# Holding two early loads back behind a VectorE count, in a kernel of attention and feed-forward on one core

## The chip, the cores and the metric

The kernel runs on 1 core of one Trainium2 chip. The metric is the device time of one execution in microseconds (us); medians of several executions are given.

## The reference, cut to what matters

```python
mod = (silu(c) @ w_mod).reshape(1, 6, 1, -1)      # sa, ca, ga, sb, cb, gb
h = layernorm(x) * (1 + ca) + sa                  # x: 2048 x 1024
x = x + ga * attention(h, k_cache, v_cache, wq, wo)   # 32 heads of 128, last 512 keys
h = layernorm(x) * (1 + cb) + sb
x = x + gb * ((silu(h @ w_gate) * (h @ w_up)) @ w_down)
```

## The kernel before

TensorE does nearly all of the work. The tokens are handled in chunks of 512. The first attention phase is a loop over steps `i`, one head of one chunk at a time: project a query head, score the previous head, apply the probabilities of the one before. In between, the other engines prepare what comes later:

- **Tile transposes.** The normalised rows of the second chunk go through four DMA transposes on SyncE's queue (steps 3 to 5). At steps 8 and 9 VectorE *modulates* the result (gain and shift). The projection at step 9 is the first to read it.
- **Units.** The output projection is done later with seven products instead of eight, which needs differences of blocks of `wo`. They are prepared in sixteen units: GpSimd loads 512 KB, VectorE makes four differences (the *sums*, two at a tick), GpSimd stores them to memory.
- **Gate columns.** The columns of `w_mod` for `ga`, two loads of 1 MB, on SyncE's queue; the products of steps 12 to 14 read them.

```python
def unit_load(end):
    ...
    T.op(Q_of[slot][0], lambda: g.dma_start(dst, src), writes=[w.b_raw, w.b_s3])   # g: GpSimd

def unit_chain(k0, k1):
    unit_load(k1)
    unit_load(k1)
    yield
    for k in range(k0, k1):
        ...            # two pairs of sums, then the store and the load of the next unit

def pre0(i):
    ...
    if i in (7, 8):
        load_wga(i - 7)                                 # gate columns
    ...
    if i in (8, 9):
        for dt in range(4 * (i - 8), 4 * (i - 8) + 4):
            modulate(hT[1], B_hT[1], dt, 0, 0, B_mode, x1_tiles)
    if i < NQ0 + 1:
        if i % 2 == 0:
            qproj(NQ0 - 1 + i // 2)                     # ends in a copy-out on VectorE
    ...
    for n, tt in enumerate(NORMS.get(i, ())):           # steps 3, 4, 5
        norm_turn(1, tt, x1_tiles, (i + n) % 2)         # normalise, then DMA transpose
    ...
    if i == 5:
        bgx.append(row_task(sc_row, B_scr, sc_bf[:, :], B_sc))

def tick0(i):
    ...
    if i == 8:
        chain[0] = unit_chain(0, HP)
    if 8 <= i < NI - 8:
        unit_tick(i)                                    # skips every fourth step, and 21 to 24
```

`T.op` puts a wait into the issuing engine's stream only where a buffer was touched before. Nothing had touched the places of the first two units, so GpSimd issues their loads as soon as it has done its own earlier work (at 43.79 us in the profile below), however late "step 8" stands in the program.

The softmax here doesn't subtract the row's maximum and nothing guards it: scores larger than these inputs give would overflow.

## Time and profile before

| | before |
|---|---|
| time, median of the 3 executions at hand | 1162.26 us (1161.74 to 1162.92) |
| span of the profiled execution | 1159.8 us |
| TensorE busy | 1143.1 us, 99% |
| VectorE busy | 817.5 us, 70% |
| GpSimd busy | 68.8 us, 6% |

First the page of the kernel before: busy time per engine, and the chain of work that ended last, as shares of the span by engine and by line. Some 16.7 us of the span are idle TensorE; one per cent of the chain is a DMA of `nsc`, the normalised rows.

```profile
PE 1143.1 (99%) x7019; PEld 588.2 (51%) x7105; DVE 817.5 (70%) x1638; ACT 532.5 (46%) x745; POOL 68.8 (6%) x137
...
PE 94%; DVE 2%; DMA 1%; ACT 1%; issue 1%; SPq 0%; POOL 0%; DVEq 0%; ACTq 0%
PE ps L272 94%; ACT arena L805 1%; DMA arena<-nsc 1%; DVE arena L835 1%; DMA arena<-in_w_mod_dram 0%; DVE arena L906 0%; PE ps L276 0%; DVE st L413 0%; SPq L310 0%; DVE arena L432 0%; SPq L341 0%; DVE arena L852 0%; ACT tmp L743 0%; DVE arena L1563 0%; ACT L1548 0%
```

The table by windows of the same profile (busy us of each engine, with the number of instructions; then granted clock, share of the DMA engines' time, GB/s). Between 40 and 60 us TensorE lacks 3.3 us, and the DMA engines are full (share 1.00).

```profile
core 0: us, PE busy (x) PEld busy (x) DVE busy (x) ACT busy (x) POOL busy (x), PEclk, DMA share, GB/s
40.00:60.00 20.00, 16.68 (x163) 10.29 (x164) 13.51 (x33) 14.52 (x23) 3.82 (x7) 1.00 1.00 221
```

The timeline of the same profile from 42 to 56 us (start, duration, engine, line, operation, count; in brackets the idle time just before and what ended it). GpSimd issues the two unit loads at 43.79 us. SyncE issues the last two tile transposes from 43.23 us, that is the very last near 44.6 us. VectorE's first modulate (L432) waits 2.10 us for a transpose to land, the copy-out of the projection (L656) stands behind it, and TensorE waits 1.97 us for that.

```profile
43.23 2.70 SPq L454 DMA_TRANSPOSE arena<-nsc  x2
...
43.79 1.69 POOL L945 DMA_DIRECT2D arena<-in_A_wo_dram  x2
...
49.73 1.00 SPq L580 DMA_DIRECT2D arena<-in_w_mod_dram  x1
...
53.60 1.38 DVE L432 TENSOR_SCALAR arena<-arena,gain,mod_bf 128x512 f16<-128x512 f16 x4 [2.10 <-DMA arena<-nsc]
...
54.90 0.69 DVE L656 CAST arena<-ps 128x512 bf16<-128x512 f32 x1
...
55.64 0.60 PE L272 MATMUL ps<-arena 128*128 128x512 f16 x2 [1.97 <-DVE arena L656]
```

The view of the transposing line in the first 60 us gives the time from issue to landing of the four tile transposes: one took 9.0 us where the median is 3.3.

```profile
DMA to landing us min/median/max: 3.1/3.3/9.0
```

The DMA view of 47 to 51 us tells who had the engines (packets, MB, share of 16 engines): q0 is GpSimd's queue with the unit loads, q1 is SyncE's with the transposes.

```profile
q0 software_dynamic: 266, 0.96, 70.1%
q1 hardware_dynamic: 787, 0.20, 35.8%
```

### The profile page before, as it was taken

To read this page: it belongs to the slowest core of one execution; us is meant where nothing else is said; L and a number is where in the kernel's file an instruction comes from. 1 tells how busy PE (TensorE), PEld (TensorE's weight loads), DVE (VectorE), ACT (ScalarE), POOL (GpSimd) and SP (SyncE) were. 2 spreads that over 40 slices of the span, in tenths; PEclk is the share of its full clock that TensorE was granted. 3 is DMA by queue.
4 is the path that set the end of the run, shared out by engine and by line. 5 is a ranking of instruction groups with operands and counts; after the bars stand their busy time and mean duration, and the time that the engine had idled before them with its cause. 6 is when DMAs were issued, how large, how long until landed. Compare 5 with 4: busy or idle time off the path is not lost.

```text
span 1159.8 us, 18164 instructions
## 1 busy us (share of the span) xinstructions
PE 1143.1 (99%) x7019; PEld 588.2 (51%) x7105; DVE 817.5 (70%) x1638; ACT 532.5 (46%) x745; POOL 68.8 (6%) x137
## 2 busy tenths in 40 slices
PE   8899999999999999999999999999999999999999
PEld 5565556654446666556444444444444444444444
DVE  4758997657576777776567898767558777776536
ACT  3866777730117777787110344454110444544110
POOL 1200221000000111111000010000000000000000
PEclk9999999999999999999999999999999999999999
DMA  9878899966906898844865232333764424234443
GB/s 326 178 188 202 217 214 219 204 169 188 261 10 170 190 205 195 212 94 108 202 192 172 78 104 73 102 81 100 209 197 143 123 74 109 73 93 131 131 162 110
DMA packets 289941, 179.98 MB, mean 155 GB/s; under 512 B 130496, under 2 KB 278080, under 8 KB 289856
## 3 DMA queue, kind: packets, MB, share of 16 engines
q1 hardware_dynamic: 226880, 92.31, 35.8%
q10 hardware_dynamic: 54336, 55.05, 14.9%
q0 software_dynamic: 8640, 31.46, 9.1%
q8 instruction: 56, 0.92, 0.3%
q14 instruction: 29, 0.24, 0.1%
HBM read 128.45 MB, written 19.92 MB: 128 GB/s over the span
## 4 chain that ended last, share of the span: by engine, by line
PE 94%; DVE 2%; DMA 1%; ACT 1%; issue 1%; SPq 0%; POOL 0%; DVEq 0%; ACTq 0%
PE ps L272 94%; ACT arena L805 1%; DMA arena<-nsc 1%; DVE arena L835 1%; DMA arena<-in_w_mod_dram 0%; DVE arena L906 0%; PE ps L276 0%; DVE st L413 0%; SPq L310 0%; DVE arena L432 0%; SPq L341 0%; DVE arena L852 0%; ACT tmp L743 0%; DVE arena L1563 0%; ACT L1548 0%
## 5 line engine op out<-in xcount | busy, mean ns | idle before, releaser
L272 PE MATMUL ps<-arena 128*128 128x512 f16 (+2 forms) x6714 | 1135.4, 329 | 13.8 <-POOL arena L406 2.2
L272 PEld LDWEIGHTS ps<-arena 128*128 128x128 bf16 (+1 forms) x6800 | 578.0, 98 | 564.8 <-DVE arena L835 6.3
L805 ACT ACTIVATE arena<-ps 128x1024 bf16<-128x1024 f32 x256 | 261.3, 1021 | 45.9 <-PE ps L272 33.9
L838 ACT ACTIVATE tmp<-ps 128x512 f32<-128x512 f32 x167 | 99.7, 597 | 297.8 <-PE ps L272 283.7
L906 DVE TENSOR_TENSOR arena<-arena 128x512 f16<-128x512 bf16 x328 | 133.5, 420 | 3.0
L835 DVE TENSOR_TENSOR arena<-ps,tmp 128x512 bf16<-128x512 f32 (+1 forms) x134 | 91.9, 686 | 49.3 <-PE ps L272 37.8
L838 ACT ACTIVATE nsc<-ps 128x512 f32<-128x512 f32 x84 | 50.1, 596 | 93.2 <-PE ps L272 90.9
L827 DVE TENSOR_TENSOR arena<-ps,rl 128x512 f16<-128x512 f32 x128 | 88.5, 691 | 4.9 <-DVE rl L824 0.5
L835 DVE TENSOR_TENSOR arena<-ps,nsc 128x512 f16<-128x512 f32 x84 | 57.4, 687 | 41.2 <-PE ps L272 29.9
L824 DVE RECIPROCAL rl<-ps 128x4 f32<-128x4 f32 x128 | 23.1, 180 | 88.0 <-PE ps L272 87.0
L1548 ACT ACTIVATE arena<-arena 128x512 f16<-128x512 f16 x84 | 49.9, 624 | 32.4 <-DVE arena L835 32.4
L1044 DVE TENSOR_TENSOR arena<-arena 128x2048 f16<-128x2048 f16 (+3 forms) x56 | 56.2, 1013 | 9.3 <-PE ps L272 8.8
L1120 DVE TENSOR_TENSOR tmp<-ps,tmp 128x512 f32<-128x512 f32 x32 | 22.1, 690 | 57.0 <-ACT tmp L838 47.3
L838 ACT ACTIVATE arena<-ps 128x512 f32<-128x512 f32 x16 | 9.6, 597 | 89.0 <-PE ps L272 89.0
L956 DVE TENSOR_TENSOR arena<-arena 128x512 f16<-128x512 bf16 x120 | 48.0, 421 | 1.9 <-DMA arena<-in_A_wo_dram 0.8
L413 DVE BATCH_NORM_STATS2 st<-x_res 128x6 f32<-128x512 bf16 x58 | 39.6, 683 | 3.9 <-DMA x_res<-in_A_x_dram 3.7
L1563 DVE TENSOR_TENSOR arena<-arena 128x512 f16<-128x512 f16 x84 | 35.1, 418 | 0.3
L1121 DVE TENSOR_TENSOR tmp<-tmp,rowb 128x512 f32<-128x512 f32 (+1 forms) x49 | 33.6, 686 | 1.7
L427 DVE TENSOR_SCALAR nsc<-x_res,mv,rstd 128x1024 f16<-128x1024 bf16 (+1 forms) x30 | 16.2, 541 | 24.1 <-DMA arena<-nsc 23.4
L603 DVE SCALAR_TENSOR_TENSOR arena<-arena 128x1024 bf16<-128x1024 bf16 x24 | 29.2, 1217 | 0.0
L1122 DVE TENSOR_TENSOR arena<-tmp,x_res 128x512 bf16<-128x512 f32 (+1 forms) x33 | 22.3, 675 | 1.1
L835 DVE TENSOR_TENSOR arena<-ps,rowb 128x512 f16<-128x512 f32 x28 | 19.3, 690 | 3.9 <-ACT rowb L838 3.4
(87 smaller groups left out, 333.9 us busy)
## 6 DMA issues: line engine op xcount, KB each, us to landing
arena<-in_A_wq_dram SPq DMA_DIRECT2D x28, 512.0 KB, 5.2
arena<-wo_sum ACTq DMA_DIRECT2D x7, 2048.0 KB, 8.7
arena<-in_B_w_gate_dram SPq DMA_DIRECT2D x28, 512.0 KB, 4.1
arena<-in_B_w_up_dram SPq DMA_DIRECT2D x28, 512.0 KB, 4.9
arena<-wd_sum ACTq DMA_DIRECT2D x8, 1792.0 KB, 7.8
arena<-in_B_w_down_dram ACTq DMA_DIRECT2D x6, 1792.0 KB, 7.2
arena<-in_A_wo_dram POOLq DMA_DIRECT2D x16, 512.0 KB, 4.9
wo_sum<-arena POOLq DMA_DIRECT2D x16, 512.0 KB, 4.7
```

The lines of the kernel that those rows point to most:

```text
L272: T.op(PE, lambda: TE.matmul(out_ap, lhsT, rhs, start=start, stop=stop, skip_group_check=skip), reads=reads, writes=[bank_buf])
L413: T.op(DVE, lambda: V.bn_stats(st_[sl][:, hf * 6:hf * 6 + 6], x_res[:, t, hf * 512:hf * 512 + 512]), reads=[B_x[t]], writes=[B_st[sl]])
L805: T.op(ACT, lambda: A.activation(ex_s[es][:, 2 * kp:2 * kp + 2, :], banks2(SCB + 2 * kp), AF.Exp, scale=att_scale), writes=[PB[SCB + 2 * k ...
L827: T.op(DVE, lambda: V.tensor_tensor(o_s[os_].rearrange("p (a b) d -> p a b d", a=2), psap(PVB * 512, [[512, 2], [130, 2], [1, P]]), rlb, A ...
L835: T.op(DVE, lambda: V.tensor_tensor(out, bank(ba), other, ADD), reads=[ob2], writes=[PB[ba], ob])
L838: T.op(ACT, lambda: A.activation(dst, bank(bk), AF.Copy), writes=[PB[bk], db])
L906: T.op(st, lambda: eng.tensor_tensor(o, a, b, op), reads=rd, writes=[wr])
L956: T.op(DVE, lambda: V.tensor_tensor(o, a, b, SUB), reads=rd, writes=[wr])
L1044: T.op(DVE, lambda: V.tensor_tensor(o, a, b, SUB), reads=rd, writes=[sb])
L1121: T.op(DVE, lambda: V.tensor_tensor(tm, tm, rw, MULT), reads=[B_row[row]], writes=[tb])
L1548: T.op(ACT, lambda: A.activation(o, s_, AF.Silu), reads=[sb], writes=[ob])
L1563: T.op(DVE, lambda: V.tensor_tensor(gu[blk][:, p, :], o, s_, MULT), reads=[sb, ob], writes=[B_gu[blk][p]])
```

## The change

The intent: keep the unit loads off the DMA engines until the tile transposes are through. They get a wait for all the work that VectorE has been given by step 8, that is, for VectorE's instruction counter to reach that point (*the count* below); it is made with a stand-in buffer that nothing else touches. The sums start at step 12 instead of 9, so that they don't wait for the later loads, and the gate columns move one step.

```diff
-            def unit_load(end):
+            def unit_load(end, ahead=()):
...
-                T.op(Q_of[slot][0], lambda: g.dma_start(dst, src), writes=[w.b_raw, w.b_s3])
+                T.op(Q_of[slot][0], lambda: g.dma_start(dst, src), reads=ahead, writes=[w.b_raw, w.b_s3])
...
             def unit_chain(k0, k1):
-                unit_load(k1)
-                unit_load(k1)
+                after = _Buf("after")
+                after.last_write = (DVE, DVE.count)
+                unit_load(k1, [after])
+                unit_load(k1, [after])
...
-                if i in (7, 8):
-                    load_wga(i - 7)
+                if i in (8, 9):
+                    load_wga(i - 8)
...
                 if i == 8:
                     chain[0] = unit_chain(0, HP)
-                if 8 <= i < NI - 8:
+                    next(chain[0])
+                if 11 < i < NI - 4:
                     unit_tick(i)
```

## The prediction

> **What bounds it now.** The page's totals: TensorE is busy 1143.1 of 1159.8 us, so all its idle time is 16.7 us; the chain that ended last is 94% TensorE matmuls. Both builds issue the same TensorE instructions in the same order, so only idle time, mostly in the first 60 us, can be won.
>
> **What goes wrong now.** The table by windows gives 3.3 us of TensorE idle between 40 and 60 us, with the DMA engines fully busy. In the timeline:
> - GpSimd issues the first two unit loads (512 KB each) at 43.79 us, waiting for nothing but its own last rstd.
> - SyncE issues the last of four transposes of a normalised tile at 44.59 us. It lands at 53.57 us: 9.0 us, against a median of 3.3 us for these four.
> - VectorE's first modulate waits 2.10 us for it and starts at 53.60 us. Behind it in VectorE's order is the copy-out of a projection (54.90 us). TensorE needs that bank and waits 1.97 us, until 55.64 us: its longest wait after the start.
>
> The DMA view of 47 to 51 us shows what was in the way: GpSimd's queue moved 0.96 MB for 70% of the 16 engines' time, the transposes' queue 0.20 MB. [...] The first gate-column load (1 MB, issued 49.73 us) comes behind in the same place.
>
> **What the change does.**
> - It removes nothing and adds one wait on GpSimd. The unit loads go from 43.8 to about 54.5 us.
> - Gate-column loads move one step, to about 52 and 56 us. They are first needed at about 66 and 70 us and take 8 us; 3 MB in flight at 230 to 390 GB/s are through by about 63 us.
> - Sums: steps 12 to 54 keep theirs; the pairs of steps 9 and 10 (0.75 to 0.87 us each on VectorE) reappear in steps 56 and 57, where VectorE idles 0.8 and 2.25 us. The last store goes from 214.9 to about 223 us; the next load into its place is at 240 us.
> - The second chain's loads (345.2 us) also wait for VectorE, but their sums start only at 353.8 us.
>
> **Size.** Without unit loads in the way the last transpose should land near 48 to 49 us. VectorE can modulate from 51.5 us, when its previous copy ends; four modulates end near 52.9, the copy-out near 53.6, just as TensorE ends its run (53.67 us). The 1.97 us go; VectorE's 2.10 us are the same delay, not added. The second four modulates still pace the next projection (waits of 0.23 to 0.59 us), so I count 1.8 to 1.9 us. After 60 us each step is TensorE-bound at 3.49 us, so nothing gives this back. I allow 0.3 us either way for transfers shifted later. All of it is on the critical path, but it is 0.16% of the time.
>
> **Predicted:** 1160.4 us, range 1159.2 to 1161.8; faster by over 2% 0.01, within 2% 0.98, slower by over 2% 0.01.
>
> **What would show it.** Right: no DMA wait before the first modulate, no TensorE wait near 2 us between 50 and 60 us, the four transposes landing in under 5 us each, unit loads issued near 54.5 us, each reciprocal after 60 us about 1.9 us earlier. Wrong: the modulate still waits for the transpose, or TensorE waits anew near 66 to 73 us for gate columns or near 215 to 245 us.
>
> **What would make it wrong.** The delay could come from the transposes' own queue; the moved transfers now overlap fully and could hold the outputs' transposes until their four-deep ring stalls VectorE; late stores could delay the output projection.

## The result, and the profile after

The changed kernel takes 1160.1 us, median of 6 (1159.86 to 1160.62); the kernel before 1162.59 us, median of 6 (1161.74 to 1164.76). The ratio is 0.9976, 95% interval 0.9963 to 0.9989. A ratio here is the mean time of one kernel's fast runs over that of the other's of the same rounds, so not quite the ratio of the medians quoted. By the 2% rule this is "same"; the interval leaves no doubt that it is faster.

The page after: the DMA of `nsc` is gone from the chain. (TensorE's busy time is not comparable between these two profiles: the one before has 86 matmul records fewer. So the 16.7 us of idle TensorE before are too many; from the 10.0 us of the profile after and the span that is 1.5 us shorter, some 11.5 us are an estimate.)

```profile
PE 1148.3 (99%) x7105; PEld 588.0 (51%) x7105; DVE 817.4 (71%) x1638; ACT 532.7 (46%) x745; POOL 68.4 (6%) x137
...
PE 96%; DVE 2%; ACT 1%; DMA 1%; issue 0%; SPq 0%; ACTq 0%; DVEq 0%
PE ps L272 96%; ACT arena L805 1%; DMA arena<-in_A_wq_dram 1%; DVE arena L835 1%; DVE arena L906 0%; DVE st L413 0%; SPq L341 0%; SPq L310 0%; PE ps L276 0%; ACT arena L618 0%; DVE arena L852 0%; ACT tmp L743 0%; DVE arena L1566 0%; ACT L1551 0%; DVE arena L827 0%
```

The timeline after, 42 to 57 us. The unit loads go out at 55.13 us, after 11.09 us of waiting for VectorE. The modulate starts at 51.62 us without a wait, right behind VectorE's previous copy, the copy-out 2 us earlier than before. TensorE's only wait left at this place is 0.46 us, for the second four modulates.

```profile
43.36 2.68 SPq L454 DMA_TRANSPOSE arena<-nsc  x2
...
51.62 1.37 DVE L432 TENSOR_SCALAR arena<-arena,gain,mod_bf 128x512 f16<-128x512 f16 x4
52.51 0.45 SPq L580 DMA_DIRECT2D arena<-in_w_mod_dram  x1
...
52.91 0.68 DVE L656 CAST arena<-ps 128x512 bf16<-128x512 f32 x1
...
55.13 1.69 POOL L945 DMA_DIRECT2D arena<-in_A_wo_dram  x2 [11.09 <-DVE arena L827]
...
55.20 3.01 PE L272 MATMUL ps<-arena 128*128 128x512 f16 x21 [0.46 <-DVE arena L432]
```

Landing of the four tile transposes, and the DMA view of 47 to 51 us, of the changed kernel. GpSimd's queue is not there; the transposes have the engines.

```profile
DMA to landing us min/median/max: 3.1/3.3/3.4
```

```profile
q1 hardware_dynamic: 1345, 0.32, 62.0%
```

The gain can be counted between two reciprocals on VectorE that end a step: from that of step 7 to that of step 9 it is 49.99 to 59.94 us before, 9.95 us, and 50.20 to 58.42 us after, 8.22 us. That is 1.73 us won. From 58.42 us on, every step is as long as before: the span is shorter by 1.5 us, as the reciprocal is earlier by 1.52 us (the profiled execution after had started 0.2 us slower).

### The profile page after: what moved, and what is told of

It is laid out like the page before. It is cut to its first block, busy times and chain, and to the rows that moved or that the text cites. A ratio compares the mean times of both kernels' runs of the same rounds, so it can differ in the third digit from the quotient of the medians.

```text
span 1158.3 us, 18250 instructions
## 1 busy us (share of the span) xinstructions
PE 1148.3 (99%) x7105; PEld 588.0 (51%) x7105; DVE 817.4 (71%) x1638; ACT 532.7 (46%) x745; POOL 68.4 (6%) x137
## 4 chain that ended last, share of the span: by engine, by line
PE 96%; DVE 2%; ACT 1%; DMA 1%; issue 0%; SPq 0%; ACTq 0%; DVEq 0%
PE ps L272 96%; ACT arena L805 1%; DMA arena<-in_A_wq_dram 1%; DVE arena L835 1%; DVE arena L906 0%; DVE st L413 0%; SPq L341 0%; SPq L310 0%; PE ps L276 0%; ACT arena L618 0%; DVE arena L852 0%; ACT tmp L743 0%; DVE arena L1566 0%; ACT L1551 0%; DVE arena L827 0%
```

## The experiments

Twelve runs were made, each but one (c3) timed beside the kernel before on the same chip; c3 repeats the kernel before, d1 the changed kernel. Chips and rounds differ, so the kernel before has several medians. The clock column counts executions whose mean granted clock was below 1.0.

| run | what differs | median us (range) | before, same rounds | ratio (95%) | clock below 1.0 |
|---|---|---|---|---|---|
| the change | | 1160.1 (1159.86-1160.62) | 1162.59 | 0.9976 (0.9963-0.9989) | 0 of 6 |
| b1_loads_sums | change without the gate move | 1161.44 (1160.51-1165.26) | 1164.02 | 0.9983 (0.9967-1.0) | 1 of 6 |
| b2_gate_only | before with the gate move | 1164.78 (1161.7-1165.25) | 1164.02 | 1.0 (0.9983-1.0017) | 3 of 6 |
| b3_no_wait | change without the count | 1164.63 (1160.45-1165.85) | 1164.02 | 1.0002 (0.9985-1.002) | 5 of 6 |
| b4_loads_only | before with the count | 1161.31 (1160.8-1165.08) | 1164.02 | 0.9988 (0.997-1.0005) | 2 of 6 |
| c1_one_early | one unit load early, one held | 1160.71 (1160.25-1161.43) | 1164.09 | 0.9975 (0.9946-1.0004) | 0 of 4 |
| c2_sp_behind | both early, SyncE's queue | 1160.67 (1159.98-1163.67) | 1164.09 | 0.9978 (0.995-1.0005) | 0 of 4 |
| c3_before_again | kernel before, one look | 1164.53 | | | 1 of 1 |
| d1_after_again | the change again | 1160.27 (1159.91-1161.95) | 1164.32 | 0.9964 (0.9938-0.9991) | 0 of 6 |
| d2_row_later | change, row task later | 1162.04 (1160.08-1166.87) | 1164.32 | 0.998 (0.995-1.0009) | 1 of 6 |
| d3_mod_earlier | change, modulates earlier | 1159.33 (1158.8-1161.21) | 1164.32 | 0.9958 (0.9932-0.9984) | 0 of 6 |
| d4_row_mod | both | 1158.9 (1158.67-1160.65) | 1164.32 | 0.9953 (0.9924-0.9981) | 0 of 6 |
| e1_stall | change with an added stall | 1167.03 (1166.32-1168.57) | 1164.51 | 1.0029 (1.0014-1.0045) | 6 of 6 |

The theory, A: the two unit loads on GpSimd's queue hold up the tile transposes. Rivals: B, the first gate-column load does it; C, it is VectorE, relieved of the sums of steps 9 and 10; D, any megabyte moving at that time would do it.

### Without the gate move: b1_loads_sums

```diff
 (the change, but)
-                if i in (8, 9):
-                    load_wga(i - 8)
+                if i in (7, 8):
+                    load_wga(i - 7)
```

> The unit loads wait and the sums move, the gate columns stay one step earlier as before. Theory A (the two unit loads on GpSimd's queue held up the tile transpose): the four tile transposes land in under 4 us each, the first modulate has no DMA wait and starts near 51.6 us, TensorE has no wait near 2 us between 50 and 60 us; time 1.5 to 2.5 us below the kernel before, as the whole change. Rival B (the first gate-column load, issued near 50 us on the transposes' own queue, held it up): last transpose still lands after 53 us, time within 0.6 us of the kernel before.

All four transposes landed in 3.1 to 3.3 us, the modulate started at 51.85 us without a DMA wait, and TensorE had no wait of over 0.7 us but the one at the start. The two reciprocals stand at 50.42 and 58.65 us: 8.23 us, as with the whole change. B falls. The time is 2.6 us below the kernel before, by medians. Its full-clock executions (1160.51 to 1162.01) are somewhat above those of the change measured elsewhere; nothing in this profile shows a cost of the early gate load, and whether the move is worth a few tenths stays open.

### The gate move alone, and the change without the count: b2_gate_only, b3_no_wait

```diff
 (b2: the kernel before, but)
-                if i in (7, 8):
-                    load_wga(i - 7)
+                if i in (8, 9):
+                    load_wga(i - 8)
 (b3: the change, but)
-                unit_load(k1, [after])
-                unit_load(k1, [after])
+                unit_load(k1)
+                unit_load(k1)
```

> Only the gate-column loads one step later; unit loads early and sums as before. Theory A: the last tile transpose still takes 7 us or more, the modulate still waits 1 to 2.5 us, time within 0.6 us of the kernel before. Rival B: transposes under 5 us, no wait, 1.5 to 2.5 us faster.

> The whole change without the count: sums from step 12 and gate columns one step later, unit loads issued near 44 us again. Theory A: stall of the modulate is back (7 us or more to landing, 1 to 2.5 us waited), time within 0.6 us of the kernel before. Rival C (taking the sums of steps 9 and 10 off VectorE made room): time like the whole change, 1.5 to 2.5 us faster.

Both are as slow as the kernel before (ratios 1.0 and 1.0002; the medians are 0.8 and 0.6 us higher, where within 0.6 us was expected). In both the last transpose is late again. The timelines show the modulate's wait, 1.83 us in b2, and in b3 only 0.42 us, below the 1 us that the expectation asked for:

```profile
55.58 1.38 DVE L432 TENSOR_SCALAR arena<-arena,gain,mod_bf 128x512 f16<-128x512 f16 x4 [1.83 <-DMA arena<-nsc]
```

```profile
52.41 1.38 DVE L432 TENSOR_SCALAR arena<-arena,gain,mod_bf 128x512 f16<-128x512 f16 x4 [0.42 <-DMA arena<-nsc]
```

Landing times of the tile transposes, b2 first, then b3:

```profile
DMA to landing us min/median/max: 3.1/3.3/8.8
```

```profile
DMA to landing us min/median/max: 3.1/4.1/7.2
```

So B and C fall as explanations of the gain: with early unit loads, neither the gate move nor the moved sums gains anything. But b3's profiled execution took 1160.45 us, as fast as the change, while its other five took 1163.83 to 1165.85 us at a clock of 0.997 to 0.999. In that profile the two reciprocals are 8.27 us apart, hardly more than with the change (8.22): with both loads early, nearly nothing was lost. The stall that I took for a fixed cost is not fixed.

### The count alone: b4_loads_only

```diff
 (the change with the gate loads at steps 7 and 8, and)
-                if 11 < i < NI - 4:
+                if 8 < i < NI - 8:
```

> The count alone: unit loads near 55 us, sums still from step 9, gate columns as before. Theory A: the transpose stall goes, but the first sum at step 9 on VectorE now waits for a load that lands near 60 us, 1 to 5 us; some of it reaches TensorE at the next copy-out, so the gain is between 0 and 1.5 us and a wait of VectorE's sums on the load shows. If moving the sums was needless: no such wait, 1.5 to 2.5 us faster.

The transposes landed in 3.3 us at most and the modulate didn't wait. But the first sum, now at 61.32 us, waited 2.33 us for a load that had gone out at 54.79 us, and TensorE paid for most of it at the next copy-out. VectorE's line first, then TensorE's:

```profile
61.32 0.89 DVE L956 TENSOR_TENSOR arena<-arena 128x512 f16<-128x512 bf16 x2 [2.33 <-DMA arena<-in_A_wo_dram]
62.12 0.68 DVE L656 CAST arena<-ps 128x512 bf16<-128x512 f32 x1
```

```profile
62.86 5.40 PE L272 MATMUL ps<-arena 128*128 128x512 f16 x35 [1.32 <-DVE arena L656]
```

So in the profile the later start of the sums saves 1.3 us at this place. The times don't show it: b4's median is 2.7 us below the kernel before, more than the 0 to 1.5 us expected (1.4 us by the ratio, whose interval includes no gain), and in the same rounds b1, with the sums moved, has 1161.44 against b4's 1161.31. That the two edits belong together is shown by the waits, not by the times.

### Half the dose: c1_one_early

```diff
 (the change, but)
-                unit_load(k1, [after])
+                unit_load(k1)
                 unit_load(k1, [after])
```

> The changed kernel, but the first of the two unit loads is issued near 44 us as before and only the second waits. Half the dose. In the changed kernel the last tile transpose lands near 48.2 us and VectorE asks for it at 51.6 us, 3.4 us of slack; the two loads together moved for 4.6 us. Theory A: one load delays the landing by about 2 to 3 us, to 50 to 51.5 us, within the slack, so no wait or under 0.5 us, TensorE loses under 0.4 us and executions at full clock take 1160 to 1160.8 us. Rival (any early unit load brings the stall): the modulate waits 1 us or more and the time is that of the kernel before.

```profile
DMA to landing us min/median/max: 3.1/3.2/6.2
```

The last transpose took 6.2 us instead of 3.3, so one load alone delays it by 2.9 us. It hurts nobody: the modulate starts at 51.69 us without a wait. The delay of 2.9 us stays within the slack of 3.4 us and is free; in the kernel before, 5.7 us of delay (9.0 less 3.3) became 2.10 us of wait, about what exceeds the slack. (Two of the four executions, 1161.11 and 1161.43 us, lie above the 1160.8 us expected.)

### The same bytes on SyncE's queue: c2_sp_behind

```diff
 (the change; the first two unit loads leave unit_chain(0, HP) and go, at step 5, to SyncE)
                     norm_turn(1, tt, x1_tiles, (i + n) % 2)
+                if i == 5:
+                    unit_load(HP, sp=True)      # T.op(Q_sp[slot], lambda: SP.dma_start(dst, src), ...)
+                    unit_load(HP, sp=True)
```

> The changed kernel, but both unit loads go out early, near 46 us, on SyncE's own queue right behind the last tile transpose instead of on GpSimd's queue. Same bytes, same time, another queue. Theory A (two queues share the engines, packets of 4096 bytes against packets of 256): behind the transposes in their own queue the loads cannot pass them, all four land in under 4.5 us, the first modulate has no wait, executions at full clock within 0.7 us of the changed kernel's 1160.1 us. Rival D (a megabyte moving at that time is enough, whatever the queue): last landing 7 us or more, the modulate waits 1 us or more.

The DMA view of 47 to 51 us and the landings of this run:

```profile
q1 hardware_dynamic: 800, 1.10, 98.9%
```

```profile
DMA to landing us min/median/max: 3.1/3.3/3.4
```

1.10 MB moved in those 4 us, about as much as in the kernel before, and the tile transposes landed in 3.4 us at most; the modulate started at 51.48 us without a wait. D falls as it was put: a megabyte on its way early is harmless when it stands behind the transposes in their queue. But it is harmless because it moves later: in the DMA records the first packet of these loads starts at 47.20 us, and the last packet of the transposes ahead of them at 47.32 us. In the kernel before the two took turns, almost packet for packet: from 47 to 49.5 us, 193 packets of 4096 bytes on GpSimd's queue and 178 of 256 bytes on SyncE's. Two more limits: the loads here were issued at 45.95 us, 2.2 us later than before, and of four executions at full clock two were over the 0.7 us allowed, 1161.17 and 1163.67 us, which this work doesn't explain.

### The kernel before, a second profile: c3_before_again

> The kernel before, unchanged, for a second profile. Theory A says the early loads always reach the transposes, so the last tile transpose takes 6 us or more again; how much of it becomes a wait may vary, between 0.3 and 2.5 us, with where the instruction fetches near 51 us fall. If it lands in under 5 us here, the first profile was a stray and theory A is in doubt.

The landing, the waits of VectorE and TensorE, and the windows:

```profile
DMA to landing us min/median/max: 3.1/3.3/10.4
```

```profile
55.03 1.38 DVE L432 TENSOR_SCALAR arena<-arena,gain,mod_bf 128x512 f16<-128x512 f16 x4 [3.48 <-DMA arena<-nsc]
...
57.07 3.24 PE L272 MATMUL ps<-arena 128*128 128x512 f16 x9 [3.34 <-DVE arena L656]
```

```profile
58.00:59.00 1.00, 0.90 (x4) 0.30 (x3) 1.00 (x4) 0.00 (x0) 0.00 (x0) 0.84 1.07 342
59.00:60.00 1.00, 1.00 (x4) 0.39 (x3) 0.19 (x2) 0.00 (x0) 0.00 (x0) 0.50 1.14 371
...
61.00:62.00 1.00, 1.00 (x8) 0.72 (x7) 0.00 (x0) 0.91 (x2) 0.00 (x0) 0.50 1.03 365
62.00:63.00 1.00, 1.00 (x15) 0.84 (x13) 0.16 (x1) 0.92 (x1) 0.00 (x0) 0.95 0.51 113
```

The transpose took 10.4 us, 7.1 more than the median of the four. Some 3.4 us of that are slack (in the changed kernel it lands near 48.2 us and is asked for at 51.6); VectorE waited 3.48 us, more than the 2.5 us expected at most, and TensorE stood for 3.34 us. Then comes something that the first profile didn't have: the clock column goes to 0.50 and stays there for 3.4 us (the trace's clock record says 3413 ns). The step in which it falls, from VectorE's reciprocal at 56.93 us to the next at 62.84 us, takes 5.91 us, in the first profile 4.45 us (55.49 to 59.94): 1.46 us more. By an estimate, half of the 3413 ns, the lower clock costs 1.7 us. Wait and clock together, 3.34 + 1.7 less the 0.46 us that the changed kernel also waits, make 4.6 us; this span is 1162.7 us against 1158.3, 4.4 us.

### A stall without any transfer: e1_stall

```diff
 (the change, and in pre0)
+                if i == 8:
+                    for _ in range(7):
+                        stats(0, 0, 0)          # a needless bn_stats; its result is not used
```

> The changed kernel with seven needless bn_stats (0.61 us apart, 4.3 us) on VectorE ahead of the first modulate; loads untouched, result unchanged. A measured stall without any transfer in the way. TensorE should wait near 4.0 us for the copy-out (4.3 less 0.3 us of slack). Theory E (a wait of over some 3 us costs more than itself, because TensorE's granted clock then halves for one window, as in the second profile of the kernel before: 0.50 for 3.4 us after a wait of 3.34 us): executions show a mean clock of 0.999 or 0.998 and take 1165 to 1166.5 us, 1.7 us more than the wait alone; the profile shows clock 0.50 for about 3.4 us after 58 us. Without that effect: clock 1.0 and 1163.6 to 1164.6 us.

The result is still correct, and the four transposes landed in 3.4 us at most. TensorE's line of the timeline, then the windows:

```profile
58.70 11.62 PE L272 MATMUL ps<-arena 128*128 128x512 f16 x65 [4.74 <-DVE arena L656]
```

```profile
56.00:57.00 1.00, 0.00 (x0) 0.00 (x0) 0.97 (x4) 0.00 (x0) 0.00 (x0) 1.00 1.01 393
57.00:58.00 1.00, 0.00 (x0) 0.00 (x0) 1.00 (x5) 0.00 (x0) 0.00 (x0) 0.50 0.08 29
...
62.00:63.00 1.00, 1.00 (x4) 0.36 (x3) 0.67 (x1) 0.00 (x0) 0.00 (x0) 0.50 0.74 209
63.00:64.00 1.00, 1.00 (x7) 0.45 (x6) 0.03 (x1) 0.81 (x1) 0.00 (x0) 0.59 0.96 336
```

The wait is 4.74 us (seven instructions were 5.0 us, not 4.3 as I had estimated), and the mean clock was below 1.0 in all six executions, for two windows of 3.413 us in the profiled one (6827 ns in the record). The profiled execution's span is 6.4 us over that of the change (1164.7 against 1158.3; by medians of different rounds, 6.9). The wait gives 4.74 less 0.46, and, by the same estimate, half of the 5.1 us at half clock in which TensorE had work 2.6 us: 6.9, so 0.5 us more than the spans show. Theory E holds in that the clock fell, at double the windows foreseen. Two long stalls of TensorE, made in different ways (3.34 us in c3, 4.74 us here), cost more than themselves: the spans are 4.4 and 6.4 us longer than the changed kernel's.

How long is long? The clock records answer more than I had asked. In every kept profile that has one, the clock changes only at whole multiples of 3.413 us from the record's start (3413, 6827 and 51200 ns are 1, 2 and 15 of them), so the span can be cut into its windows. TensorE's busy time in the emptiest ones, and the clock that followed:

| profile | window, us | TensorE busy | clock in the next window |
|---|---|---|---|
| e1 | 53.58 to 57.00 | 0.39 us, 11% | 0.50 |
| c3 | 55.27 to 58.69 | 1.52 us, 44% | 0.50 |
| b2 | 8.80 to 12.21 | 1.62 us, 47% | 0.50 |
| e1 | 57.00 to 60.41, at half clock | 1.71 us, 50% | 0.50 |
| c3 | 51.86 to 55.27 | 1.87 us, 55% | 1.00 |
| kernel before | 54.24 to 57.65 | 1.91 us, 56% | 1.00 |
| d2 | 103.79 to 107.20 | 2.14 us, 63% | 1.00 |

Apart from the start and the end of the program, no other window is under 60% busy. So here a window in which TensorE was busy for half the time or less was followed by half clock, and one with 55% or more was not. In these records the clock goes by how much idle time falls into one window, not by how long the wait is: the 3.34 us of c3 were split over two windows, 55% and 44% busy, and only the second was followed by half clock. An estimate from these numbers: where TensorE is otherwise busy, a stall of under 1.5 us (45% of 3.413) should be safe, one of over 3.4 us not (at least 1.7 us of it, half, fall into one window), and in between it depends on where the windows fall. This was read from the records afterwards; no run was made to test it.

### Does this explain the times of the kernel before?

The kernel before had 40 timed executions with recorded clocks in four sets of rounds. In 28 of them the mean clock was below 1.0 (median 1164.7 us, 1163.25 to 1170.66), in 12 it was 1.0 (median 1161.6 us, 1160.25 to 1162.08). With b2 and b3, kernels with both unit loads early on GpSimd's queue had the lower clock in 36 of 52 timed executions; the kernels without had it in 4 of 50, the deliberate stall left out. That the lower clock comes from this stall was seen in one profile (c3) and made on purpose in another (e1); for the other executions it is inferred from the counts. It is not the only cause: the profiled execution of b2 had its halved window at the start of the kernel, 12.2 to 15.6 us, after the window of 47% in the table, in which no single wait was over 0.91 us. By the table, in the full-clock executions of the kernel before the stall should have been short, or split between two windows; the times alone can't tell which. Either way, comparing full-clock executions alone would leave out the part of the gain that comes through the clock.

### Further versions: d1 to d4

The changed kernel still has waits of TensorE of 0.24 and 0.51 us (for the exponentials on ScalarE at steps 6 and 7) and 0.46 us (for the second modulates).

```diff
 (d3 and d4)
-                if i in (8, 9):
-                    for dt in range(4 * (i - 8), 4 * (i - 8) + 4):
+                if i in (7, 8):
+                    for dt in range(4 * (i - 7), 4 * (i - 7) + 4):
 (d2 and d4)
-                if i == 5:
+                if i == 9:
                     bgx.append(row_task(sc_row, B_scr, sc_bf[:, :], B_sc))
```

> The changed kernel again, to stand beside the next three on one chip. All theories: four tile transposes under 5 us each, no DMA wait before the modulate, TensorE's remaining waits between 40 and 60 us near 0.2, 0.5 and 0.5 us; executions at full clock 1159.8 to 1160.8 us.

> The changed kernel with the row broadcast of silu(c) begun at step 9 instead of 5: its eight small ScalarE scalings (0.33 us each) no longer stand before the exponentials of steps 6 and 7, for which TensorE waits 0.24 and 0.51 us. Expected 0.5 to 1.2 us below the changed kernel at full clock, and these two waits gone or under 0.2 us; if ScalarE is not what paces these steps, no gain.

> The changed kernel with the modulates at steps 7 and 8 instead of 8 and 9. Transposes land near 48.2 us, the first modulate would start near 49.0 us in VectorE's idle 1.2 us of step 7, the second four near 51.6 us, so the projection at step 9 finds all of its input: the wait of 0.46 us and the small ones behind it go. Expected 0.4 to 0.9 us below the changed kernel at full clock; no gain if the transposes land later than 49 us.

> Both of the last two. Expected sum: 0.9 to 2.0 us below the changed kernel at full clock, near 1158.7 us, the fastest of all.

d1 confirms the change in other rounds, with 4.1 us between the medians this time (one execution, 1161.95 us at full clock, lies above the 1160.8 us expected). d3's median is 0.9 us below d1's, the upper end of what was expected, though the two ranges overlap: with the transposes landing near 48.2 us, the modulates fit into VectorE's idle time of step 7. TensorE's timeline of d3 shows one unbroken run where d1 had the wait of 0.46 us:

```profile
49.06 6.09 PE L272 MATMUL ps<-arena 128*128 128x512 bf16 x54 [0.51 <-ACT arena L805]
55.62 11.90 PE L272 MATMUL ps<-arena 128*128 128x512 f16 x86 [0.46 <-DVE arena L432]
```

```profile
48.70 17.45 PE L272 MATMUL ps<-arena 128*128 128x512 bf16 x140 [0.51 <-ACT arena L805]
```

d2 is a miss. The two small waits became one of 0.69 us, but its profiled execution then shows a new wait of 2.28 us at 105.06 us: a sum on VectorE had waited 3.37 us for a unit load at step 20. It need not come from d2's edit: at the same step of b2, without that edit, a sum waits 2.33 us and TensorE 1.24 us, and in the profiles of d3 and of the kernel before it waits 0.39 and 0.15 us. d2's other executions scatter from 1160.08 to 1166.87 us; why, its single profile doesn't settle. d4 has the lowest median, 1158.9 us, 1.4 us below d1 in the same rounds, and beats both kernels; five of its six executions lie between 1158.67 and 1159.82 us, below all six of d1. Whether d2's part adds anything to d3's there is not shown (0.4 us between the medians, ranges that overlap).

## Why the prediction was right

- **What bounds the kernel: right.** 99% TensorE; only idle time was to be won, and after 58 us the steps stayed as they were.
- **Who stood in the way: right, and shown.** The count alone frees the transposes (b1, b4), and without it nothing is gained (b2, b3). The prediction rested here on the DMA view of 47 to 51 us: 0.96 MB of GpSimd's queue, 70.1% of the 16 engines' time, against 0.20 MB of SyncE's, 35.8%. c2 adds what decided it: on one queue, behind the transposes, the same loads start when they are nearly through (first packet at 47.20 us, the transposes' last at 47.32); on a second queue they take turns with them (193 packets against 178 from 47 to 49.5 us, in the kernel before).
- **"The 1.97 us go", 1.8 to 1.9 us counted: right in the profile,** 1.73 us measured between the two reciprocals, and 1.52 us at each later one, because the profiled execution after had started 0.2 us slower. TensorE's idle time between the two reciprocals fell from 2.12 to 0.46 us; those 0.46 us are the wait for the second modulates, which the prediction had kept but took at 0.1 to 0.2 us.
- **Parts that move: right.** Loads at 55.13 us (54.5 said), gate loads at 52.51 and 56.09 us (52 and 56), last store at 222.24 us (223), no new wait at either place named. What the prediction passed over is why the sums had to move: in b4's profile leaving them costs 2.33 us of VectorE wait and 1.3 us of TensorE wait, though b4's times don't show it.
- **The time: right,** 1160.4 said, 1160.1 measured, range 1159.2 to 1161.8.
- **What was mis-sized: the gain, in executions that the prediction hadn't seen.** It took the wait for a constant 1.97 us and the three times at hand, 1162.26 us, for the level of the kernel before. With the same two early loads TensorE's wait was 0.3 us (b3), 1.7 us (b2), 1.97 us and 3.34 us (c3), and in c3 the clock added an estimated 1.7 us. So the medians differ by 2.5 us in the first rounds and by 4.1 us in d1's, instead of 1.9. The time of the changed kernel was foreseen because the change removes the unsteady part; the difference was not. There was luck in it too: the profile at hand had full clock and a wait of 1.97 us, and the three times at hand (1161.74 to 1162.92 us) lie near the later full-clock ones, while 28 of the 40 later executions had a lower clock. The same 1.9 us taken from a median of 1164.3 us, that of d1's rounds, would have given 1162.4 us, outside the range.

One more step is open: why the wait varies with the same loads. The trace's DMA records show, in the kernel before, two instruction fetches (16384 and 8192 bytes, 1.2 and 2.0 us) at 51.3 and 51.4 us, with transposes of 256-byte packets in flight of which some took up to 1.5 us instead of 0.02; in the changed kernel the fetches come at 48.6 and 49.1 us, when the four tile transposes have landed. In c3 they come at 53.1 and 53.3 us, with packets as slow. So a delayed transpose may meet the fetches too, and be delayed again. Four profiles fit this: the last transpose had landed and the modulate began 2.9 and 2.6 us after the last packet of the unit loads in the kernel before and in c3, where a fetch of 2.03 and 1.89 us ran in between, but 1.2 and 1.3 us after it in b2 and b3, where the fetch came later or took 0.54 us. The loads themselves were not steady either: their packets ran for 4.8 us in the kernel before, and for 6.5, 6.2 and 4.5 us in c3, b2 and b3; why is open. No run moved a fetch by itself, so none of this is shown as the cause.

## What to carry to other kernels

A transfer whose buffers are free goes out when its issuer gets there, not where it stands in the program (here at 43.79 us, when the reciprocal that ends step 7 came only at 49.99); if it then shares the DMA engines with a small transfer that the critical chain awaits (here one of 3.3 us took 9.0), give it a wait that lets the small one through, and move its consumers by as much. Look at the slack of the awaited transfer (here 3.4 us): a delay of 2.9 us, below it, was free, and one of 5.7 us, above it, cost VectorE a wait of 2.10 us. When times of one kernel scatter, look at the granted clock: a stall that left TensorE idle for half or more of a 3.4 us window was followed here by half clock, and in c3 the step in which that fell was 1.46 us longer than in the first profile, so taking the stall away also took away most of the scatter (in d1's rounds 1160.25 to 1170.66 us before, 1159.91 to 1161.95 us after).
